# Score visits of three pairs instead of two in the first columns of a fused attention and feed-forward kernel

## The chip, the cores and the metric

The kernel runs on one core of a Trainium2 chip. The metric is the device time of one execution in microseconds (us); it is given as the median of five runs. A profile of one further execution shows each engine: PE is TensorE (its weight loads are listed apart as PEld), DVE is VectorE, ACT is ScalarE, POOL is GpSimd, and SP only issues DMAs here.

## The reference

Inputs: u and v with 8 batches x 3008 x 256, z with 8 x 3008 x 64, weights w_in (256 x 2048) and w_out (2048 x 256). Cut to what is computed:

```python
def _attn_ref(u, v, z):
    scores = (1.0 / S) * np.matmul(z, z.transpose(0, 2, 1))
    attn = np.maximum(scores, 0.0) ** 2
    return u * np.matmul(attn, v)

def _moe_ref(x, w_in, w_out):
    h = x @ w_in
    return (h * np.cos(h)) @ w_out

reference = _moe_ref(_attn_ref(u, v, z).reshape(B * S, D), w_in, w_out)
```

The scores of a batch are symmetric, and squared ReLU is applied to each of them by itself.

## The kernel before

**Tiling.** The 3008 tokens of a batch are 23 blocks of 128 and one of 64. Four blocks make a column of 512, so a batch has NC = 6 columns. The score tile (b, c, R) holds the scores of the four key blocks of group R against the 512 queries of column c. It is made in two pairs, p = 0 for the blocks k = 0, 1 and p = 1 for k = 2, 3. z is only 64 wide, so the transposed z (zT) holds two neighbouring blocks one above the other, and the two matmuls of a pair (L271) read opposite halves of the rows: they are half-high, 64x128, and run side by side. Each writes one PSUM bank of 512 fp32 columns. The pool ps_w (L196) has six such banks, used in rotation; the first transposes of z, the scores, the first matmuls of the second stage (L516) and its results (L533) all take their banks from it. The pool ps_acc has the other two, one for each half of the 256 values.

**From scores to products.** s_squares empties a bank with a ReLU into the fp16 ring rt (L191, three buffers of a pair each), and DVE squares a pair into one of 18 stores (L309). In the first three columns of the first batch, which the code calls direct, ACT does the ReLUs (L307), but DVE takes the last block of each tile, and one more in the very first (L305). Then av_chunk (L362) multiplies blocks of v with the squared scores into the two acc banks, three blocks or six full-high matmuls at a time. The last half block of 64 tokens is half-high too (av_half, L339) and is issued within a visit. finish (L389) multiplies the finished acc with the transposed u on DVE and so makes x, the input of the second stage.

**The second stage** goes by tiles of 512 tokens: h_quantum (L516) makes 128 of the 2048 features, ACT takes the cosine (L520), DVE multiplies (L523), and y_quantum (L533) multiplies with w_out.

**Direct columns.** Later columns reuse the symmetry: a tile with R < c is the transposed tile (R, c), turned by a DMA on SP (turn_s, L321), and part of the products goes through sums (product, L482). The direct columns need none of that, since all six tiles of each are computed. They start with the diagonal, in the order R = c, c+1, ... around the six groups. TURNS (L247) lists when those of their tiles that later columns need are turned.

**What sets the order.** Every piece of work is put on a list with a planned time: `at(t, rank, f)`. One column is U = 8 units. The list is sorted and run through once, and that is the order in which PE's matmuls execute: `chain` ties each to the one before. The order on the other engines is the framework's, within the dependencies. A score visit (s_visit) issues all matmuls of its pairs, with av_half between where one is due, and then their evictions. The loop at L572 plans the visits of the direct columns; planned times also give each tile's store its lifetime (L596). The av chunks of column c are planned at c x 8 + q + 0.5, q = 0 to 7 (the last at 7.45 instead of 7.5).

**DMAs.** POOL issues the loads and SP the transposing DMAs, each queue in its own order. A load, and a transposition of u or z, is held until the matmul that came last on the list before it has executed (`hold`, L116). In the stretch in question these are: turn_u of column 0 (planned at 0.7, behind the first av chunk), turn_u of column 1 (1.5), load_u of column 2 (2.0), the quarters of w_in from 7 to 13 and of w_out at 19, 21, 23 and 25, and at 24 the z of the next batch.

**The start.** Eight matmuls on zeros (L716) run while z comes in. z is transposed on PE in three groups of eight blocks (first_z_turn, L222), planned at -30, -2.5 and 0.8, and copied to zT by ACT (L227, the first two groups) or DVE (L229, the third). The third group holds the blocks from 16 on, which the visits of R = 4 and 5 read.

Of the kernel before, what the change touches and what calls it, by code (L numbers as in the profile page):

```python
# [14 lines left out]
def kernel(  # L15
# [25 lines left out]
    NC = NJ // K  # L41
# [5 lines left out]
    U = 8  # L47
# [47 lines left out]
    slots = [kpool.tile([P, K * CW], FP16, name=f"s{i}") for i in range(NSLOT)]  # L95
    vsum = [kpool.tile([P, 4, 2, P], FP16, name=f"vsum{R}") for R in range(NW)]
    w_in16 = kpool.tile([P, NDH, Dff], FP16, name="w_in16")
# [50 lines left out]
    def load_v(b, g):  # L148
        t = vs(b, g)
        n, full, rest = rows(v, b, g)  # L150
        load(t[:, 0:n, :], full)
        if rest is not None:
            for p0 in (0, JLAST):
                load(t[p0:p0 + JLAST, n, :], rest)
# [12 lines left out]
    def load_u(b, c):  # L167
        r0 = c * CW
        n = min(K, (S - r0) // P)
        st = ust[c % 2]  # L170
        for dh in range(NDH):
            ds = slice(dh * P, (dh + 1) * P)
            load(
                st[:, dh, 0:n, :],
                u[b, r0:r0 + n * P, ds].rearrange("(j p) d -> p j d", p=P))
            if n < K:
                load(st[0:JLAST, dh, n, :], u[b, r0 + n * P:S, ds])
# [56 lines left out]

    def direct(b, c, R):


        return b == 0 and c <= 2

    def triangle(b, c, R):  # L240

        return R == c and (b, c) > (0, NC // 2)

# [14 lines left out]

    def s_matmuls(b, c, R, p):


        zt = zT[b % 2]
        banks = {}
        diagonal = triangle(b, c, R)
        for k in ((0, 1), (3, 2) if diagonal else (2, 3))[p]:
            s0 = k if diagonal else 0
            lo = 1 if k in ((1, 2) if diagonal else (1, 3)) else 0
            h = slice(lo * dqk, (lo + 1) * dqk)
            j0 = c * K + 1 - lo
            sp = ps_w.tile([P, CW], FP32, name="w")  # L270
            chain(nc.tensor.matmul(  # L271
                sp[:, s0 * P:], zt[h, R * K + k + 1 - lo, :],
                zt[h, j0 + s0:j0 + K, :].rearrange("p j w -> p (j w)"),
                start=True, stop=True))
            banks[k] = sp
        return banks
# [286 lines left out]
    scores = []  # L563
    when = {}
    for b in range(B):
        pairs = [(b, c, R, p) for c, R in groups for p in range(2)]
        for i in range(0, len(pairs), NV):
            some = [pr for pr in pairs[i:i + NV] if not direct(*pr[:3])]
            t = b * span - lead + span * i / len(pairs)
            if some:  # L570
                scores.append((2 * math.floor(t / 2) + 1.2, some))
        for c in range(NC):  # L572
            if direct(b, c, c):
                for i in range(NC):
                    R = (c + i) % NC
                    scores.append((c * U + 4 * i / 3 - 3.1, [(b, c, R, 0), (b, c, R, 1)]))
    for t, some in scores:
        for pr in some:
            when[pr[:3]] = max(t, when.get(pr[:3], t))
# [23 lines left out]
    for b in range(B):  # L603
        for R in range(NW):
            at(b * span + (TSUM[R] if b else 3 * U + 1 + 1.5 * R), 2, lambda b=b, R=R: v_sums(b, R))
        for c in range(NC):
# [4 lines left out]
            first, last = (0.6, 6.93) if d else (HALF[c] if W else 1.0, 7.3)  # L611
# [13 lines left out]
            elif W:  # L625
# [8 lines left out]
                for o, what in PLAN[c]:  # L634
                    for piece in what.split():
# [12 lines left out]
                        for j in part:  # L648
                            R = j // K
# [8 lines left out]
            for o, size in places:  # L658
                part = blocks[n:n + size]
                if part:  # L660
                    first, end = n == 0 and not W, n + size >= len(blocks)
                    at(o, 2, lambda b=b, c=c, part=part, first=first, end=end:
                       av_chunk(b, c, part, first, end))
                    for j in part:
                        R = j // K
# [6 lines left out]
    for m in range(NT):  # L672
        b, i = divmod((m + 1) * TW - 1, S)
# [10 lines left out]
    for b in range(B):  # L684
        t = b * span
        if b == 0:
            for g in range(NG):
                at(-100 + g, 0, lambda g=g: first_z_load(g))
                at((-30, -2.5, 0.8)[g], 0, lambda g=g: first_z_turn(g))
            first = [lambda: load_v(0, 0), lambda: load_u(0, 0), lambda: load_v(0, 1),  # L690
                     lambda: load_v(0, 2), lambda: load_u(0, 1)]
# [67 lines left out]
```

## Time and profile before

| | |
|---|---|
| time, median of 5 runs | 1214.65 us (1213.68 to 1214.69) |
| the profiled execution | 1221.56 us, of it the span from first to last instruction 1219.4 us |
| PE busy | 1208.2 us, 99% of the span |
| DVE busy | 1020.1 us, 84% |
| ACT busy | 831.5 us, 68% |
| POOL busy | 145.9 us, 12% |
| mean granted clock of TensorE | 0.997 |
| the visits' matmuls, L271, whole kernel | 684, 90.4 us |
| ReLUs on ACT of full tiles, L307 | 489, 613 ns each |
| squares of a pair on DVE, L309 | 254, 688 ns each |

The busy share of an engine counts time in which any instruction of it is under way. Neighbouring instructions overlap at their ends, so the distance from start to start is shorter than a duration: ACT starts ReLUs of 0.60 us every 0.48 us, DVE starts instructions of 0.68 us every 0.60 us. A line of a timeline or a chain has the start in us, the length in us, the engine, the source line, what it writes from what, and how many instructions are merged; in brackets stands the idle time before it and what ended that.

### The profile page before, as it was taken

To read this page: it belongs to the slowest core of one execution; us is meant where nothing else is said; L and a number is where in the kernel's file an instruction comes from. 1 tells how busy PE (TensorE), PEld (TensorE's weight loads), DVE (VectorE), ACT (ScalarE), POOL (GpSimd) and SP (SyncE) were. 2 spreads that over 40 slices of the span, in tenths; PEclk is the share of its full clock that TensorE was granted. 3 is DMA by queue.
4 is the path that set the end of the run, shared out by engine and by line. 5 is a ranking of instruction groups with operands and counts; after the bars stand their busy time and mean duration, and the time that the engine had idled before them with its cause. 6 is when DMAs were issued, how large, how long until landed. Compare 5 with 4: busy or idle time off the path is not lost.

```text
span 1219.4 us, 22944 instructions
## 1 busy us (share of the span) xinstructions
PE 1208.2 (99%) x8421; PEld 767.6 (63%) x8421; DVE 1020.1 (84%) x1995; ACT 831.5 (68%) x1741; POOL 145.9 (12%) x201
## 2 busy tenths in 40 slices
PE   8989999999999999999999999999999999999998
PEld 3346666666666666666666666666666666666666
DVE  8878988889888898888888888887888888888875
ACT  6757766677676777767767677776777767767545
POOL 3310101001010010100101001010010111100000
PEclk9989999999999999999999999999999999999999
DMA  9997968779687796858977679586695857956411
GB/s 151 189 153 115 141 104 123 124 120 142 98 121 120 127 136 108 121 111 125 128 121 122 110 120 154 103 124 107 113 154 102 132 102 111 160 94 120 73 31 49
DMA packets 484225, 145.02 MB, mean 119 GB/s; under 512 B 432400, under 2 KB 484112, under 8 KB 484112
## 3 DMA queue, kind: packets, MB, share of 16 engines
q1 hardware_dynamic: 356448, 88.73, 45.3%
q0 software_dynamic: 100400, 29.77, 24.8%
q10 hardware_dynamic: 27264, 25.06, 6.4%
q8 instruction: 66, 1.08, 0.4%
q14 instruction: 47, 0.39, 0.1%
HBM read 60.29 MB, written 24.64 MB: 70 GB/s over the span
## 4 chain that ended last, share of the span: by engine, by line
PE 94%; issue 2%; DMA 2%; DVE 1%; ACT 1%; POOL 0%; POOLq 0%; ACTq 0%; DVEq 0%
PE w L533 26%; PE w L516 25%; PE acc L482 18%; PE acc L362 18%; PE w L271 6%; DMA w_out<-in_moe_w_out_dram 1%; PE acc L339 1%; DMA v<-in_v_dram 1%; ACT rt L307 0%; PE w L716 0%; DVE g L523 0%; POOL zst L121 0%; DVE s L309 0%; DVE x L389 0%; ACT zT L227 0%
## 5 line engine op out<-in xcount | busy, mean ns | idle before, releaser
L520 ACT ACTIVATE c<-w 128x512 f16<-128x512 f32 x752 | 436.8, 620 | 262.2 <-PE w L516 215.2
L523 DVE TENSOR_TENSOR g<-w,c 128x512 f16<-128x512 f32 x752 | 492.4, 683 | 65.2 <-ACT c L520 63.5
L533 PE MATMUL w<-w_out,g 128*128 128x256 f16 x3008 | 448.9, 273 | 3.8 <-DMA w_out<-in_moe_w_out_dram 3.8
L516 PE MATMUL w<-x,w_in 128*128 128x512 f16 x1504 | 445.7, 379 | 0.0
L533 PEld LDWEIGHTS <-g 128*128 128x128 f16 x3008 | 294.5, 98 | 195.2 <-issue 4.4
L362 PE MATMUL acc<-s,v 128*128 128x512 f16 (+1 forms) x1024 | 293.0, 381 | 0.1
L307 ACT ACTIVATE rt<-w 128x512 f16<-128x512 f32 x489 | 253.1, 613 | 43.9 <-PE w L271 43.9
L309 DVE TENSOR_TENSOR s<-rt 128x1024 f16<-128x1024 f16 x254 | 172.7, 688 | 85.9 <-ACT rt L307 84.7
L516 PEld LDWEIGHTS <-w_in 128*128 128x128 f16 x1504 | 147.1, 98 | 73.5 <-issue 3.9
L482 PE MATMUL acc<-s,vsum 128*128 128x256 f16 (+1 forms) x1184 | 154.6, 270 | 0.2 <-DVE q L498 0.2
L121 POOL DMA_DIRECT2D ust<-in_u_dram x112 | 81.2, 731 | 563.5 <-PE acc L362 535.2
L362 PEld LDWEIGHTS <-v 128*128 128x128 f16 x1024 | 95.9, 98 | 79.6 <-issue 32.7
L482 PEld LDWEIGHTS <-vsum 128*128 128x128 f16 x1184 | 114.9, 98 | 18.4 <-issue 3.3
L482 PE MATMUL acc<-s,v 128*128 128x256 f16 (+1 forms) x888 | 115.1, 270 | 0.4 <-DVE x L389 0.4
L482 PEld LDWEIGHTS <-v 128*128 128x128 f16 x888 | 83.7, 98 | 19.8 <-issue 12.1
L451 DVE TENSOR_TENSOR s<-s,s 128x1024 f16<-128x1024 f16 (+1 forms) x148 | 92.8, 668 | 3.6 <-PE acc L482 3.6
L271 PE MATMUL w<-zT 64*128 64x512 f16 (+3 forms) x684 | 90.4, 359 | 2.4 <-ACT zT L227 1.6
L540 ACT ACTIVATE ob<-w 128x256 f32<-128x256 f32 x188 | 71.1, 378 | 12.6 <-PE w L533 12.6
L288 ACT ACTIVATE rt<-w 128x512 f16<-128x512 f32 (+3 forms) x176 | 62.8, 449 | 11.8 <-PE w L271 11.8
L121 POOL DMA_DIRECT2D v<-in_v_dram x40 | 31.2, 785 | 299.5 <-PE acc L482 146.5
L389 DVE TENSOR_TENSOR x<-acc,ut 128x512 f16<-128x512 f32 (+7 forms) x112 | 64.1, 596 | 2.2 <-PE acc L362 2.1
L441 DVE TENSOR_TENSOR s<-s 128x512 f16<-128x512 f16 (+1 forms) x148 | 60.0, 411 | 1.9
(37 smaller groups left out, 360.3 us busy)
## 6 DMA issues: line engine op xcount, KB each, us to landing
out_dram<-ob ACTq DMA_DIRECT2D x92, 256.0 KB, 2.4
ust<-in_u_dram POOLq DMA_DIRECT2D x80, 128.0 KB, 4.4
v<-in_v_dram POOLq DMA_DIRECT2D x16, 512.0 KB, 6.4
s<-s SPq DMA_TRANSPOSE x249, 4.4
v<-in_v_dram POOLq DMA_DIRECT2D x8, 448.0 KB, 9.3
zst<-in_z_dram POOLq DMA_DIRECT2D x14, 128.0 KB, 5.0
ust<-in_u_dram POOLq DMA_DIRECT2D x16, 96.0 KB, 5.0
w_in<-in_moe_w_in_dram POOLq DMA_DIRECT2D x4, 256.0 KB, 5.9
```

The costliest lines, as they stand in the source:

```text
L121: hold(nc.gpsimd.dma_start(dst, src))
L271: chain(nc.tensor.matmul(sp[:, s0 * P:], zt[h, R * K + k + 1 - lo, :], zt[h, j0 + s0:j0 + K, :].rearrange("p j w -> p (j w)"), start=True, ...
L307: nc.scalar.activation(rt[:, i, :], banks[k], AF.Relu)
L309: ins = nc.vector.tensor_tensor(t.rearrange("p s k w -> p k s w")[:, 2 * p:2 * p + 2], rv, rv, ALU.mult).ins
L362: chain(nc.tensor.matmul(acc[:, 0:wn], vs(b, j // G)[:, j % G, nh * P:(nh + 1) * P], a, start=(start and n == 0), stop=(last and n == len( ...
L451: after(nc.vector.tensor_tensor(dst, src, sub, ALU.subtract).ins, before[-1], NOSYNC)
L482: chain(nc.tensor.matmul(acc[bank][:, cols], lhs[:, k, :], rhs[:, k, :] if old else rhs[:, :, k * P:(k + 1) * P], start=(n in (1, 5) and i ...
L516: chain(nc.tensor.matmul(hp, w_in16[:, k, ft * P:(ft + 1) * P], x[:, k, :], start=(k == 0), stop=(k == NDH - 1)))
L520: nc.scalar.activation(c16, hp, AF.Sin, bias=math.pi / 2.0, scale=inv_s2)
L523: nc.vector.tensor_tensor(gs[(m, ft // FG)][:, ft % FG, :], hp, c16, ALU.mult)
L533: chain(nc.tensor.matmul(ys[m][:, 0:D], gs[(m, f4)][:, ft % FG, ts * P:(ts + 1) * P], w_out16[:, ft, :], start=(ft == 0), stop=(ft == NFT ...
L540: nc.scalar.activation(obs[m][:, i, :], ys[m][:, 0:D], AF.Copy, bias=0.0, scale=inv_s2)
```

## The change

The visits of the direct columns are no longer planned one tile at a time. All their pairs are put into one row, column after column, and cut into visits: the first has two pairs, the next ten have three, the last two have two.

```diff
-        for c in range(NC):
-            if direct(b, c, c):
-                for i in range(NC):
-                    R = (c + i) % NC
-                    scores.append((c * U + 4 * i / 3 - 3.1, [(b, c, R, 0), (b, c, R, 1)]))
+    pairs = [(0, c, (c + i) % NC, p) for c in range(NC) for i in range(NC) for p in range(2)]
+    pairs = [pr for pr in pairs if direct(*pr[:3])]
+    first = [0, 2, *range(5, 33, 3), 34]
+    for i, j in zip(first, first[1:] + [len(pairs)]):
+        scores.append((2 * i / 3 - 3.6, pairs[i:j]))
```

The planned times and contents that follow, with a pair written as (column, group, p):

| before | | after | |
|---|---|---|---|
| -3.10 | (0,0,0) (0,0,1) | -3.60 | (0,0,0) (0,0,1) |
| -1.77 | (0,1,0) (0,1,1) | -2.27 | (0,1,0) (0,1,1) (0,2,0) |
| -0.43 | (0,2,0) (0,2,1) | -0.27 | (0,2,1) (0,3,0) (0,3,1) |
| 0.90 | (0,3,0) (0,3,1) | 1.73 | (0,4,0) (0,4,1) (0,5,0) |
| 2.23 | (0,4,0) (0,4,1) | 3.73 | (0,5,1) (1,1,0) (1,1,1) |
| ... every 1.33 | one tile each | ... every 2.00 | three pairs each |
| 18.23 | (2,0,0) (2,0,1) | 17.73 | (2,0,0) (2,0,1) |
| 19.57 | (2,1,0) (2,1,1) | 19.07 | (2,1,0) (2,1,1) |

That makes 18 visits before and 13 after, of the same 36 pairs. The first av chunk (0.5) stands behind the third visit in both; the third group of z transposes (0.8) and the second chunk (1.5) come between the third and the fourth visit after the change, and on both sides of the fourth before it. The last half block of each direct column is still issued within a visit: those planned at 6.23, 12.90 and 19.57 before, at 5.73, 11.73 and 17.73 after. The last visit stood behind the chunk of 19.5 and directly ahead of the first h_quantum (20.0); it now stands ahead of that chunk. Nothing else is edited: the turns, the loads, the chunks and the numbers of banks and buffers keep their planned times and sizes.

## The prediction

> **What bounds the kernel now.** I read the page first, then the stretch that the change touches. The page's slices say that TensorE (PE) is busy nearly all the time, with one dent.
>
> ```profile
> PE   8989999999999999999999999999999999999998
> PEclk9989999999999999999999999999999999999999
> ```
>
> The dent (third slice, 61 to 91 us) lies behind the stretch that the change edits. A table of stretches splits that: 8.6 to 10.4 us is the start, 10.40 to 46.38 us runs from the first av chunk to the first quantum of the second stage (L516).
>
> ```profile
> 8.60:10.40 1.80, 1.06 (x4) 0.20 (x5) 1.80 (x4) 1.80 (x5) 1.59 (x4) 1.00 1.64 181
> 10.40:46.38 35.98, 35.90 (x192) 12.86 (x192) 32.42 (x54) 23.98 (x47) 7.21 (x10) 1.00 1.30 171
> ```
>
> The columns after the length are PE, its weight loads, VectorE (DVE), ScalarE (ACT), POOL, the granted clock and the DMA share. In the first row ACT and DVE are full and PE is not: the first scores wait for their evictions. In the second PE works 35.90 of 35.98 us, DVE 32.42, ACT 23.98: PE sets the pace, so a PE saving counts there, while DVE has 3.6 us to spare. The chain of waits shows what a visit costs PE:
>
> ```profile
> 12.37 0.54 PE w L271 x4
> 12.91 1.40 PE acc L362 x6
> 14.31 0.54 PE w L271 x4
> ...
> 53.82 1.29 PE acc L362 x6
> ...
> 116.88 0.75 PE w L271 x6
> ```
>
> Four half-high matmuls (two pairs) take 0.54 us, six take 0.75: a pair costs 0.21 and a visit 0.54 - 2 x 0.21 = 0.12 besides. The six full-high matmuls behind a visit take 1.40 us, six between other full-high ones 1.29: 0.11 more on leaving. So one visit costs 0.23 us of PE beyond its pairs.
>
> The timeline of the start, by engine:
>
> ```profile
> 8.93 3.08 ACT L307 ACTIVATE rt<-w 128x512 f16<-128x512 f32 x6
> 9.11 1.36 PE L271 MATMUL w<-zT 64*128 64x512 f16 x4 [0.54 <-ACT zT L227]
> 10.40 1.47 PE L362 MATMUL acc<-s,v 128*128 128x512 f16 x6
> 13.11 0.81 DVE L229 COPY zT<-w 128x1024 f16<-128x1024 f16 x2
> 24.11 1.28 DVE L389 TENSOR_TENSOR x<-acc,ut 128x512 f16<-128x512 f32 x2
> ```
>
> ACT empties a bank every 0.48 us (9.42, 9.90, 10.37 in narrower windows); DVE starts an instruction every 0.60 us; the first av chunk begins at 10.40.
>
> **The change part by part.**
>
> *Fewer visits.* 18 become 13, so five times 0.23 us: -1.15. The second and third visit stand side by side before the first chunk both before and after, so all five fall behind 10.40, where PE is full. Bounds: -1.15, and 0 should PE wait there instead.
>
> [...]
>
> *Two pairs moved ahead of the first chunk.* Before: three visits, six pairs. After: 2 + 3 + 3 = eight. Behind the chunk PE is spared 2 x 0.21 = -0.43. In front the third visit now holds (2,1), (3,0), (3,1), and all six banks are taken by the second. Its last matmul writes the bank that the ReLU of block (2,0), second half, reads: the fifth ReLU in the row of six from 8.93, so free at 8.93 + 4 x 0.48 + 0.60 = 11.45. Before, the last matmul before the chunk waited for the second ReLU, 8.93 + 0.48 + 0.60 = 10.01, and the chunk started 0.39 later. Add 0.35 (a visit's last pair to the next chunk): the chunk starts at 11.80, +1.40. Bounds: +0.95 if one ReLU goes to another place in ACT's order, +2.0 if one more stands ahead. The v transfer, awaited until 10.40 now, is no bound then.
>
> *What waits behind it.* Next on PE are the nine transposes of the third z group (L222), one chunk, and the visit of R = 4, which needs the zT copy on DVE (L229). The chain gives 11.80 + 1.40 + 0.50 + 1.30 = 15.00 for that visit (14.31 now). DVE, at 0.60 a start, has rt, square, square, rt, square after the rt of 11.31, so it is at 14.3 when the transposes, done about 13.85, want their copy: the copy ends at 15.0 if it goes next and at 15.6 if a square goes first. Nobody but PE waits for it. 0 to +0.6; I take +0.3, as nothing in the trace orders the two.
>
> *Bank and ring reuse in the steady part.* A visit is followed by two or three chunks, so the next starts 0.75 + 1.40 + 1.30 = 3.45 us later and finds all six banks last used by the visit before. A visit of kind A (two pairs of one block, one of the next) needs five ReLUs on ACT: from 0.42 us after its start (17.48 to 17.90 in the timeline), 0.42 + 4 x 0.48 + 0.60 = 2.94. Kind B (one, then two) gives DVE two bank-emptying maxima (L305) and three squares, 5 x 0.60 = 3.0 us, its last bank empty by 3.3 at the worst order. Both are under 3.45 plus the 0.4 until the third pair's turn: 0, and up to 0.3 a visit if DVE is behind. The rt ring (L191, three buffers) is just as deep as a visit; its third buffer is released by 3.65 and wanted at about 5.3.
>
> *End of a column.* The x multiplications (L389, 2 x 0.60) hold the two acc banks that the next chunk wants. For column 0 the third square of the visit before is ready at the same moment (2.95 us after its start) as the first x; if it goes first, PE waits 0.3. For column 1 x goes first, and a wait of 0.15 us seen now (the chain's chunk at 39.07, due at 38.92) goes. -0.15 to +0.3, taken as +0.05.
>
> *DMAs and queues.* The moved visits issue no DMA: the turns of these columns have times of their own (L247), and none precedes its squares. The gates shift: turn_u of column 0 on SP opens at the end of the first chunk, 11.90 now, 13.3 then. Behind it on SP stands turn_u of column 1, which starts only at 20.48 since its u has not landed; the transposed u is wanted at 24.11 and the staging buffer was free at 20.66. So 0. POOL's weight loads wait for matmuls that move by the net shift. The planner's slots (L587), worked through for the new times, are each reused only after the reader of the old content. The last direct visit moves ahead of one chunk (19.07 for 19.57); the next visit (21.2) still waits for the product of the last quantum before it: 0.
>
> Sum: -1.15 - 0.43 + 1.40 + 0.3 + 0.05 = **+0.17 us**. The profiled execution took 1221.56 us, its span 1219.4 and 2.2 around it; so 1221.7 for it. The median of the runs shown is 1214.65, 0.6% less, and the same sum gives 1214.8. From the bounds of the start, the copy and the column's end, this case runs from -1.15 - 0.43 + 0.95 - 0.15 = -0.8 to -1.58 + 2.0 + 0.6 + 0.3 = +1.3: 1213.9 to 1216.0.
>
> **The rivals.** The dent decides what could be larger. PE waits there for the last quarter of w_out, and its clock falls:
>
> ```profile
> 74.59 1.01 PE L533 MATMUL w<-w_out,g 128*128 128x256 f16 x4 [3.77 <-DMA w_out<-in_moe_w_out_dram]
> ...
> 75.40 4.90 PE L362 MATMUL acc<-s,v 128*128 128x512 f16 x11
> ```
>
> Eleven matmuls take 4.90 us and not 11 x 0.216 = 2.4, and four take 1.01 and not 0.44, so the halved clock costs about 3.0 and the dent 3.77 + 3.0 = 6.8 us. The profiled run is 1221.56 - 1214.65 = 6.9 us longer than the median; so the runs that count probably lack the dent.
>
> *Rival 1, slower: the clock falls at the start.* Place: 8.6 to 11.8 us, where PE, waiting for banks, now does six half-high matmuls (6 x 0.21 = 1.3 of 3.2 us). In the dent the clock fell about 3 us after PE's last matmul, and in 8.6 to 10.4 at 1.06 of 1.80 us it stayed 1.00. It decides when the sparse stretch counts as idle over its whole length. Price 3.0: 1214.8 + 3.0 = 1217.8. Against it: PE is never idle for over 0.6 us there.
>
> [...]
>
> *Rival 2, faster: the transfers shift.* SP issues the turned tiles one after another from 20.48 to 75.2 us, and w_out shares the DMA engines with them. The turn of (0,0,3) is ready some 1 us earlier relative to the turn_u that now goes ahead of it; if the order flips, SP uses its idle time before 20.48 for it, all later ones come up to 4.5 us (one issue, 21.82 to 26.45) sooner, and the dent's wait goes. If the median runs have the dent: 1214.8 - 6.8 = 1208.0. Against: the 6.9 us above, and the turn_u is still ready first by about 1 us.
>
> *Rival 3, slower: the dent comes into runs that lack it.* PE is early, or w_out late, by enough: 1214.8 + 6.8 = 1221.6. For it: the profile shows how little separates the two; against: the gate of w_out moves along with PE.
>
> *Rival 4: the full saving, start hidden.* If the start costs only its lower bound and no copy or x is late: 1213.9, within the same class.
>
> **How the numbers follow.** 0.2% is 2.4 us, about what a measurement of this kernel can tell from no change. Forecast with Rival 4: 0.50. Rival 1: 0.12. Rival 3: 0.10. DVE late at each of the eight three-pair visits from 1.73 on (0.3 x 8 = +2.4 and the sum, 1217.2): 0.09. Rival 2: 0.10, and other shifts of the transfers to the fast side 0.09. Faster 0.19, same 0.50, slower 0.31. The range takes in Rival 1 and the late DVE and stops short of Rivals 2 and 3: 1212.0 to 1218.6; the likeliest case alone has 1213.9 to 1216.0.
>
> **What would show it.** After the change: 13 rows of L271 before the first L516, ten of them 0.75 us; the first L362 at about 11.8; the first L516 at 46.2 to 47, with PE still full from the first chunk on; clock 1.00 until the dent. A first chunk before 11.3 or a clock under 1.00 at 12 us refutes the start; L271 rows over 0.9 us behind 15 us refute the bank reuse; a w_out wait of another length makes the prediction wrong whatever the rest does.

## The result, and the profile after

The changed kernel takes 1216.19 us (median of 26 runs, 1215.45 to 1217.46) where the kernel before takes 1214.66 (44 runs): the ratio is 1.0012, 95% interval 1.0007 to 1.0018. That is 1.5 us more, and within the 0.2% that was set as no change. The profiled execution took 1216.23 us with a span of 1214.2.

The page after, the two slice rows that showed the dent, and the rows of the table of stretches that answer to the two of before (start; first av chunk to first L516):

```profile
PE   8999999999999999999999999999999999999998
PEclk9999999999999999999999999999999999999999
```

```profile
6.20:11.70 5.50, 4.10 (x25) 1.33 (x25) 5.06 (x9) 4.94 (x9) 4.73 (x7) 0.94 1.43 170
11.70:48.83 37.13, 36.01 (x189) 13.90 (x188) 33.12 (x54) 23.30 (x46) 6.50 (x9) 0.96 1.33 184
```

The two rows of stretches list, behind the length, the busy time of PE, its weight loads, DVE, ACT and POOL, then the granted clock and the DMA share. The dent is gone from this execution. But the first chunk comes at 11.70 us, the first L516 at 48.83 where it was 46.38, and PE now has 1.1 us idle in the second stretch (36.01 of 37.13) and a mean clock of 0.96. The chain of waits shows the start of it:

```profile
10.61 1.16 PE w L271 x4
11.76 2.67 PE acc L362 x6
14.44 0.59 PE w L222 x9
15.03 1.29 PE acc L362 x6
16.32 0.75 PE w L271 x6
17.07 2.69 PE acc L362 x12
```

The first chunk's six matmuls take 2.67 us and not 1.40: 0.445 each, half speed. From 15.03 on everything has its old pace, and visits of six take 0.75. The clock in half-microsecond stretches (PE busy, clock, DMA share, GB/s) has the limits:

```profile
10.50:11.00 0.50, 0.39 (x3) 1.00 1.55 180
11.00:11.50 0.50, 0.50 (x2) 0.58 1.49 195
...
14.00:14.50 0.50, 0.50 (x5) 0.51 1.44 197
14.50:15.00 0.50, 0.50 (x10) 1.00 1.46 199
```

Halved from about 11.1 to 14.5 us. Three waits stand in the steady part, in PE's timeline:

```profile
26.39 0.82 PE L271 MATMUL w<-zT 64*128 64x512 f16 x6
27.51 2.75 PE L362 MATMUL acc<-s,v 128*128 128x512 f16 x12 [0.30 <-DVE x L389]
...
40.33 0.82 PE L271 MATMUL w<-zT 64*128 64x512 f16 x6
41.66 2.75 PE L362 MATMUL acc<-s,v 128*128 128x512 f16 x12 [0.52 <-DVE x L389]
44.35 0.61 PE L271 MATMUL w<-zT 64*128 64x512 f16 x4
45.26 0.39 PE L339 MATMUL acc<-s,v 64*128 64x512 f16 x2 [0.30 <-DVE s L309]
45.58 1.47 PE L362 MATMUL acc<-s,v 128*128 128x512 f16 x6
```

The first two are chunks that begin a column and find acc not yet read. The third is the half block of column 2. By the starts, each of these visits takes longer to its chunk than the 0.75 us of an undisturbed one: 27.51 - 26.39 = 1.12, 41.66 - 40.33 = 1.33 and 45.58 - 44.35 = 1.23. So PE loses 0.37, 0.58 and 0.48.

### The profile page after: what moved, and what is told of

Its sections match the earlier page's. It is cut to its first block, busy times and chain, and to the rows that moved or that the text cites. A ratio compares the mean times of both kernels' runs of the same rounds, so it can differ in the third digit from the quotient of the medians.

```text
span 1214.2 us, 22940 instructions
## 1 busy us (share of the span) xinstructions
PE 1205.5 (99%) x8421; PEld 767.3 (63%) x8421; DVE 1021.0 (84%) x1995; ACT 831.3 (68%) x1741; POOL 145.8 (12%) x201
## 4 chain that ended last, share of the span: by engine, by line
PE 98%; DVE 0%; DMA 0%; ACT 0%; issue 0%; ACTq 0%; DVEq 0%
PE w L533 27%; PE w L516 27%; PE acc L362 19%; PE acc L482 19%; PE w L271 6%; PE acc L339 1%; DMA g<-in_z_dram 0%; DVE s L309 0%; DVE x L389 0%; DVE rt L305 0%; ACT rt L307 0%; ACTq L209 0%; ACT zT L227 0%; DVE zst L217 0%; ACT c L520 0%
## 5 line engine op out<-in xcount | busy, mean ns | idle before, releaser
L516 PE MATMUL w<-x,w_in 128*128 128x512 f16 x1504 | 445.7, 379 | 0.0
L516 PEld LDWEIGHTS <-w_in 128*128 128x128 f16 x1504 | 147.0, 98 | 73.2 <-issue 3.1
```

Of the source, the lines that this page charges most:

```text
L516: chain(nc.tensor.matmul(hp, w_in16[:, k, ft * P:(ft + 1) * P], x[:, k, :], start=(k == 0), stop=(k == NDH - 1)))
```

## The experiments

The expectations weigh three theories of where the loss arises. A puts it at the start and in the halved clock there, B in the visits of three pairs of the steady part, C behind the first L516, in the transfers. (From ends on, the letters stand for what each expectation says.) One table first, since all runs are read by it. Times are from each profile's PE timeline: the first visit, the distances from there to the visit of R = 4 and from that to the first L516, and what is left of the span behind the first L516.

| profile | first visit | to R = 4 | to first L516 | behind it | median of its executions |
|---|---|---|---|---|---|
| before, second profile | 6.47 | 7.60 | 32.14 | 1165.4 | 1214.65 |
| before, third profile | 6.78 | 8.24 | 32.14 | 1165.3 | 1214.55 |
| changed | 6.22 | 10.03 | 32.58 | 1165.4 | 1216.19 |
| changed, second profile | 6.34 | 10.05 | 32.58 | 1165.3 | 1216.37 |
| warm | 6.78 | 9.02 | 32.58 | 1165.3 | 1215.89 |
| start_two | 6.31 | 7.72 | 33.20 | 1165.4 | 1215.76 |
| rest_two | 6.78 | 8.43 | 32.14 | 1172.6 | 1215.96 |
| ends | 6.59 | 10.10 | 31.28 | 1165.3 | 1215.41 |
| col_two | 6.78 | 7.60 | 32.09 | 1165.8 | 1216.27 |
| col_two_ends | 6.50 | 7.60 | 31.50 | 1165.5 | 1213.60 |
| best | 6.78 | 7.60 | 31.50 | 1165.5 | 1214.88 |
| before_wout | 6.78 | 8.24 | 32.14 | 1165.3 | 1214.78 |

The last column but one answers theory C at once: unless PE waits for w_out (rest_two), the time behind the first L516 is 1165.3 to 1165.8 us in every profile. What the front loses or gains arrives at the end, within 0.5 us. The distances repeat to about 0.1 us where the clock does the same, while the executions of one kernel scatter by 1 to 2 us and more, so I read the causes from the profiles and use the times only as a check.

**before_again**: nothing edited.

> The kernel before once more, for a second profile. If the halved clock and the wait for w_out behind 70 us belong to the one profiled execution only, the span here is about 1212.5 us, the clock stays 1.00 from 70 to 90 us and PE waits under 0.5 us for w_out; if they are in every execution, the span is about 1219 us. Time 1214.7 us, ratio 1.000 either way.

Span 1211.6 us, clock 1.00 throughout, no wait for w_out; ratio 1.0007 (0.9996 to 1.0017). The dent of the first profile belonged to that execution: of the 154 executions of before that stand beside these runs, five took over 1218 us. It is no part of the difference.

**warm**: ten full-high matmuls more, between the score pairs of the second and third visit.

```diff
+    def warm(n):
+        acc = ps_acc.tile([P, CW], FP32, name="acc")
+        for i in range(n):
+            chain(nc.tensor.matmul(acc, ident, zT[0][:, 0:4, :]..., start=True, stop=True))
...
+            if pair in WARM:
+                warm(WARM[pair])
```

> The changed kernel with ten more full-high matmuls (zT against the identity, into an acc bank that nobody reads) put between the score pairs of the second and third visit, where PE waits for banks. Theory A (the start costs the time, and 1.4 us of it is the clock that halves from 11.2 to 14.5 us in a stretch with little PE work): the clock stays 1.00 there, the first av chunk's six matmuls take 1.3 to 1.4 us and not 2.67, the visit of R = 4 stands 8.7 us behind the first visit and not 10.1, time 1214.8 us, 1.4 less than the changed kernel. Theory B (the loss arises from visits of three pairs in the steady part) and theory C (it arises behind the first L516, in the transfers): the start may come earlier, the time stays at 1216.2.

PE's timeline of it, from the last of the added matmuls (L330):

```profile
10.99 0.82 PE L330 MATMUL acc<-zT,ident 128*128 128x512 f16 x3
11.75 0.61 PE L271 MATMUL w<-zT 64*128 64x512 f16 x4
12.29 1.47 PE L375 MATMUL acc<-s,v 128*128 128x512 f16 x6
```

The first chunk (now L375) is at full speed, the clock is 1.00 in every stretch, and R = 4 comes 1.0 us sooner behind the first visit (9.02 for 10.03, where 8.7 was expected). The added matmuls cost some of it, as PE is busy all of 7.8 to 11.2 us, and PE also waits for the zT copy, which DVE runs behind two squares here:

```profile
15.80 0.82 PE L271 MATMUL w<-zT 64*128 64x512 f16 x6 [0.25 <-DVE zT L229]
```

The stretch to the first L516 is the same 32.58. The gain shows in the profile; in the medians it is only 0.3 us and not the expected 1.4 (1215.89, ratio to before 1.0016, 1.0008 to 1.0025). One profile can't show that the added matmuls kept the clock, since that of rest_two kept it without them; the executions lean that way, with 10 of 11 at a mean clock of 1.000 against 17 of 37 of the changed kernel.

**start_two** and **rest_two** undo one half each.

```diff
 start_two
-    first = [0, 2, *range(5, 33, 3), 34]
+    for i in range(4):
+        scores.append((4 * i / 3 - 3.1, pairs[2 * i:2 * i + 2]))
+    first = [*range(8, 33, 3), 34]
 rest_two
+    first = [0, 2, 5, 8]
+    for i, j in zip(first, first[1:]):
+        scores.append((2 * i / 3 - 3.6, pairs[i:j]))
+    for n in range(4, 18):
+        c, i = divmod(n, NC)
+        scores.append((c * U + 4 * i / 3 - 3.1, pairs[2 * n:2 * n + 2]))
```

> The changed kernel, but the first four visits as before (one tile of two pairs each, R = 0 to 3, at the planned times of before); three pairs from R = 4 on. Theory A: clock 1.00 at the start, the visit of R = 4 stands 7.7 us behind the first visit as before, the first L516 40.2 us behind it (39.7 before, 42.6 in the changed kernel, 0.5 of the difference from waits at the columns' ends), time 1215.1. Theory B: time 1216.2, as in the changed kernel. Theory C: anything from 1214.7 to 1216.2 that does not follow the first L516.

> The start of the changed kernel (visits of 2, 3 and 3 pairs before the first av chunk), and one tile of two pairs a visit from R = 4 on, as before. Theory A: the clock halves at the start as in the changed kernel, the visit of R = 4 stands 10.1 us behind the first, the first L516 42.1 us, time 1215.7. Theory B: time 1214.7, as before.

start_two: the start is as before (7.72, clock 1.00). The rest takes 33.20 and not the expected 32.5: the visit of R = 4 now stands one chunk behind the visit of R = 3 and waits for its banks.

```profile
14.03 0.82 PE L271 MATMUL w<-zT 64*128 64x512 f16 x5
15.10 0.37 PE L271 MATMUL w<-zT 64*128 64x512 f16 x1 [0.25 <-ACT rt L307]
15.41 2.76 PE L362 MATMUL acc<-s,v 128*128 128x512 f16 x12
```

1.38 us for a visit of 0.75, so 0.63 lost with only one chunk between two visits of three pairs. Ratio 1.0011 (1.0002 to 1.0020).

rest_two: the rest is as before to the hundredth (32.14). Its profiled start kept the clock (1.00 in every half microsecond from 7 to 15 us), against what I expected, and so gives the price of the start without it:

```profile
7.87 0.84 PE L271 MATMUL w<-zT 64*128 64x512 f16 x4
9.25 2.83 PE L271 MATMUL w<-zT 64*128 64x512 f16 x8 [0.54 <-ACT zT L227]
12.01 1.47 PE L362 MATMUL acc<-s,v 128*128 128x512 f16 x6
```

The chain of waits ahead of that chunk ends on ACT's fifth ReLU in the row that starts at 9.07:

```profile
10.98 0.68 ACT rt L307
11.66 0.04 issue
11.71 0.37 PE w L271
12.08 1.40 PE acc L362 x6
```

The first chunk is 12.01 - 6.78 = 5.23 us behind the first visit (3.76 before), R = 4 8.43 behind it. With the clock halved the changed kernel needs 10.03 and 10.05: 1.6 us more. In its executions the two show apart: five with a mean clock of 1.000 took 1214.8 to 1215.5, six with 0.998 or 0.999 took 1215.9 to 1216.8. Ratio 1.0007 (0.9994 to 1.0020). Theory B, that the loss is all in the steady part, falls: the rest alone undone doesn't restore the start, and the median stays at 1215.96 where B expected 1214.7.

**after_again**: the changed kernel once more.

> The changed kernel once more, for a second profile and more executions. [...]

The profile is again one with the halved clock; in 6 of its 11 and 14 of the 26 earlier executions the mean clock is below 1.000, as it is in 12 of the 110 executions of before beside the experiments. Ratio 1.0021 (1.0012 to 1.0030).

PE's work ahead of the drop doesn't explain by itself why rest_two kept the clock with the same first three visits. Times in us:

| profile | the stretch | PE busy in it | clock in it | clock behind it |
|---|---|---|---|---|
| changed | 7.8 to 11.2 | 2.12 of 3.40 | 0.98 | 0.50 (11.1 to 14.5) |
| changed, second profile | 7.8 to 11.2 | 2.46 of 3.40 | 1.00 | 0.53 (11.2 to 14.6) |
| before, second profile | 7.8 to 11.2 | 2.64 of 3.40 | 1.00 | 1.00 (10 to 20) |
| warm | 7.8 to 11.2 | 3.40 of 3.40 | 1.00 | 1.00 (11.2 to 14.6) |
| rest_two | 8.5 to 12.0 | 2.49 of 3.50 | 1.00 | 1.00 (12.0 to 15.0) |

The clock fell behind a stretch 0.62 and 0.72 full and held behind 0.78 and 1.00, but in rest_two it also held with 0.71. The profiles differ in the time before: the eight transposes ahead of the first visit take 1.06 us from 4.62 in rest_two and 0.62 from 4.50 in the changed kernel. Whether that decides it isn't shown.

**ends** takes the three waits away.

```diff
-            first, last = (0.6, 6.93) if d else (HALF[c] if W else 1.0, 7.3)
+            first, last = (2.0 if c == 2 else 0.6, 6.93) if d else (HALF[c] if W else 1.0, 7.3)
...
-            s_squares(*pair, banks)
+            if pair in LATE:        # (0, 1, 3, 0), (0, 2, 4, 0)
+                late.append((pair, banks))
+            else:
+                s_squares(*pair, banks)
...
             ended[:] = [ins]
+            while late:
+                s_squares(*late.pop())
```

> The changed kernel with two edits at the ends of columns: the last pair of the visit ahead of the end of columns 0 and 1 is squared behind the x multiplications, not ahead of them, and the half block of column 2 is issued in a later visit (21.2, not 17.73). Theory A (PE's waits there are DVE's order: 0.30 and 0.51 us for x, 0.55 at the half block): these three waits go, the stretch from the visit of R = 4 to the first L516 is 31.2 us and not 32.6, and the time is 1.3 less than the changed kernel's, 1214.9. Theory B (the waits cover something that is late anyway, such as the banks of the next visit): the stretch shortens by under 0.5, time 1215.8 or more.

The stretch is 31.28 and the three waits are gone. DVE's timeline ahead of column 1's end, first in the changed kernel, then in ends, where the line of x is L395:

```profile
38.85 1.29 DVE L309 TENSOR_TENSOR s<-rt 128x1024 f16<-128x1024 f16 x2 [0.18 <-ACT rt L307]
40.32 0.69 DVE L309 TENSOR_TENSOR s<-rt 128x1024 f16<-128x1024 f16 x1 [0.18 <-ACT rt L307]
40.93 1.28 DVE L389 TENSOR_TENSOR x<-acc,ut 128x512 f16<-128x512 f32 x2
42.13 1.27 DVE L305 TENSOR_SCALAR rt<-w 128x512 f16<-128x512 f32 x2
43.33 1.88 DVE L309 TENSOR_TENSOR s<-rt 128x1024 f16<-128x1024 f16 x3
```

```profile
39.05 1.29 DVE L309 TENSOR_TENSOR s<-rt 128x1024 f16<-128x1024 f16 x2 [0.17 <-ACT rt L307]
40.26 1.28 DVE L395 TENSOR_TENSOR x<-acc,ut 128x512 f16<-128x512 f32 x2
41.45 0.68 DVE L309 TENSOR_TENSOR s<-rt 128x1024 f16<-128x1024 f16 x1
```

In the changed kernel DVE is held at 40.32 by a square that waits for ACT, with x behind it in DVE's order; x then pushes the next maxima to 42.13 and their squares to 43.33, and the half block of column 2 reads one of these. In ends the late square no longer stands ahead of x. Against rest_two the stretch is 0.86 shorter with four visits fewer and the 0.15 us wait of before gone, so a visit less is worth (0.86 - 0.15) / 4 = 0.18 us, or 0.21 when the 0.12 that a visit at 30.27 waits is allowed for. Ratio 1.0014 (0.9999 to 1.0029): by the profile 1.3 us of the loss, in the times less, as three of its eleven executions took over 1218 us.

**col_two** and **col_two_ends** keep the start and column 0 as they were and use three pairs from column 1 on; the second also squares late as in ends. (Two small edits go along: the turn of (0,2,3) comes at 15.76, behind its tile, and a store's lifetime is counted from its own visit.)

```diff
-    first = [0, 2, *range(5, 33, 3), 34]
+    for i in range(NC):
+        scores.append((4 * i / 3 - 3.1, pairs[2 * i:2 * i + 2]))
+    first = [*range(12, 36, 3)]
     for i, j in zip(first, first[1:] + [len(pairs)]):
-        scores.append((2 * i / 3 - 3.6, pairs[i:j]))
+        scores.append((min(2 * i / 3 - 2.27, 19.07), pairs[i:j]))
```

> Column 0 as before (six visits of two pairs), columns 1 and 2 in visits of three: 14 visits for 18, with the start untouched. Theory A (a visit costs PE 0.23 us besides its pairs, and only the start and the columns' ends take this back): clock 1.00 at the start, the visit of R = 4 stands 7.7 us behind the first; four visits less give 0.92 back and the waits for x cost 0.66 more than before, so the first L516 stands 39.5 us behind the first visit (39.7 before), time 1214.4. Theory B (visits of three pairs cost PE time of their own): over 40.2 us, time 1215.2 or more.

> The same as col_two, with the last pair ahead of the end of columns 0 and 1 squared behind x. Theory A: no wait for x, four visits less (0.92) and the 0.15 us wait of before gone, so the first L516 stands 38.7 us behind the first visit, and the time is 1213.6, 1.0 less than before. Theory B: over 39.7 us behind it, time 1214.7 or more.

The first L516 stands 39.69 and 39.10 us behind the first visit (39.74 before). The start is untouched in both. col_two has the x waits (0.30 twice); col_two_ends has none, and misses its expected 38.7 mainly by the last visit, which has one chunk ahead of it and takes 1.13 us for 0.82. So four visits fewer bring 0.64 us in the profile. The times don't follow: ratios 1.0018 (1.0008 to 1.0027) and 0.9998 (0.9989 to 1.0007).

**col_two_ends_b** and **before_third**: repeats.

> col_two_ends once more, since its first interval (0.9989 to 1.0007) doesn't tell it from the kernel before. Theory A: the first L516 stands 0.6 us earlier behind the first visit than before (39.1 against 39.7), the time behind it is 1165.4 as in all undisturbed profiles, so the executions are 0.6 us shorter: 1213.0 where those of before are 1213.6, ratio 0.9995. If the earlier first L516 is given back behind it, the ratio is 1.000 or more.

> The kernel before a third time, for a profile of an execution of about 1214.65 us: its executions gather near 1213.6 and near 1214.65, and the second profile was one of 1213.68. If the 1.05 us lie ahead of the first L516, that comes at 47.2 us and not at 46.2 with 1165.4 us behind it; if they lie behind, it comes at 46.2 with 1166.4 behind it.

col_two_ends_b came out at 1.0021 (1.0003 to 1.0039). Its profile has the first L516 39.09 behind the first visit as expected, but also a wait (total, times, longest):

```profile
PE w L542 <- DMA w_out<-in_moe_w_out_dram: 4.9, 1, 4.9
```

and 1173.1 us behind the first L516: the dent again, in 5 of its 12 executions by their time (over 1220 us). Theory A's expectation of 0.9995 was wrong.

before_third explains the two groups of before. PE's timeline:

```profile
4.72 0.95 PE L222 MATMUL w<-ident,zst 128*128 128x128 f16 x7
6.78 1.03 PE L271 MATMUL w<-zT 64*128 64x512 f16 x4 [1.10 <-ACT zT L227]
7.75 1.04 PE L222 MATMUL w<-ident,zst 128*128 128x128 f16 x8
...
47.16 1.47 PE L516 MATMUL w<-x,w_in 128*128 128x512 f16 x6
```

The first visit takes 1.03 us and not 0.60, and the eight transposes behind it 1.04, where the changed kernel's second profile has 0.62. The first chunk, at 11.18, has its usual 1.47, so the slow pace ended before it. The first L516 comes at 47.16, 0.95 later than in the second profile, with 1165.3 behind it. That is the distance between 1213.68 and 1214.65, the two profiled executions; that all executions of before gather near 1213.6 and 1214.65 by how long the slow pace lasts is inferred from these two and the one of before_wout (first visit 1.03 us too, 1214.77).

**best** and **before_wout**: the last quarter of w_out ahead of the z loads on POOL, in col_two_ends and in before.

```diff
-                at(19 + 2 * q, 0, lambda q=q: load_w_out(q))
+                at(19 + 1.6 * q, 0, lambda q=q: load_w_out(q))
```

> col_two_ends with the quarters of w_out planned 1.6 units apart and not 2, so that POOL issues the last one ahead of the five z loads (some 4 us earlier). Theory A (an earlier first L516 is given back in some executions because PE then reaches the last quarter of w_out before it has landed, and the wait halves the clock): no wait for w_out, no execution of 1220 us, the first L516 at 39.1 behind the first visit, 1165.4 behind that, and executions near 1213.0 to 1214.2. Theory B (the long executions have another cause): executions of 1218 us and more remain as frequent as in col_two_ends (6 of 23).

> The kernel before with the same earlier quarters of w_out alone. Theory A: the executions of 1218 us and more go, the others stay at 1213.6 to 1215.1, median 1214.5, so the gain of the other run is its own. Theory B: no difference to before, long executions included.

POOL's timeline of best has it in the new order:

```profile
57.78 0.75 POOL L121 DMA_DIRECT2D w_out<-in_moe_w_out_dram x1 [3.03 <-PE w L271]
58.52 3.87 POOL L121 DMA_DIRECT2D zst<-in_z_dram x5
```

One of 12 executions took over 1218 us (6 of 23 in col_two_ends), none of 11 in before_wout, where the kernel before itself has only 5 of 154. That leans to theory A, but these are few, and the one that is left speaks against it. Ratios 1.0003 (0.9992 to 1.0014) and 0.9998 (0.9990 to 1.0007): no version tried here is shown to beat the kernel before.

## Why the prediction was right, and where it was not

The class and the range held: +0.17 us was forecast and +1.5 measured, a little beyond the +1.3 at which the likeliest case ended. Some of that is luck: the range was wide enough to take in Rival 1, and a clock drop that the sum left out came with about half of its price. By the prediction's own signs the start went otherwise, since the clock was 0.50 at 12 us, and the first L516 came at 48.83 and not at 46.2 to 47. Term by term, the distances of the profiles against the working:

- *Fewer visits, -1.15.* Right in kind, a little large: 0.18 to 0.21 us a visit for the 0.23 taken, so about -1.0. Once two chunks stood between visits, PE lost little to DVE's pace or to banks (one wait of 0.12 us in ends).
- *First chunk, +1.40.* Right: 5.23 - 3.76 = +1.47 in rest_two, 5.29 in the second profile of the changed kernel, from ACT's row of ReLUs as worked out. (In the first profile, 5.48, the cast of z came late, and the chain runs through a maximum on DVE instead.)
- *zT copy, +0.3.* 0: DVE's order has the copy ahead of the square, and neither the two profiles of the changed kernel nor that of rest_two, at full clock, shows PE waiting for it. In warm, with the squares first, PE waits 0.25, close to the +0.3.
- *Columns' ends, +0.05.* The step that failed. Measured 0.37 and 0.58 for x and 0.48 at the half block, less the old 0.15: +1.3. For column 0 the square went first, the case priced at 0.3. For column 1 I let x go first, and it was indeed ready first: ends shows it starting at 40.26, 2.76 behind its visit at 37.50, which from the changed kernel's visit at 37.31 is 40.07, ahead of the square of 40.32. But the square stood ahead of it in DVE's order, and x started behind it, at 40.93. And I carried the delay no further than x: the maxima of the next visit are tied behind x, their squares come later still, and the half block, issued two chunks on, reads one of them.
- *Rival 1, the halved clock.* It was put at 0.12 and 3.0 us. It came in about 54% of the executions (14 of 26 and 6 of 11, by a mean clock below 1.000), and costs 1.6 us at the same first visit (10.03 to 10.05 against 8.43). The price was taken from the dent, where the slow stretch lasted 6.8 us; here it lasts 3.4, so about half of that is lost. My argument against it, that PE is never idle for over 0.6 us there, was true (0.55 at most in both profiles) and decided nothing: PE was busy 2.46 of the 3.40 us from 7.8 to 11.2 in the second profile, and the clock fell. No run here shows what makes it fall.
- *Rivals 2 and 3, the dent.* Not needed for this result. The time behind the first L516 is the same in both kernels whenever the dent is absent, and of the 37 executions of the changed kernel one took over 1218 us. That the median runs of before lack the dent was right.

Summed from the profiles, the changed kernel reaches its first L516 0.83 us later by the start's banks, 1.6 by the clock and 0.44 by the rest (waits +1.3, four visits -0.85), less 0.25 for an earlier first visit: 2.6, as against the second profile of before (48.83 - 46.21). Against the third it is 1.7. The 1.5 of the medians is less than both, because both profiles of the changed kernel have the clock drop and not all executions do: 17 of the 37 have a mean clock of 1.000 and a median of 1215.73, 1.1 above before, and the other 20 have 1216.50, 1.8 above. So the banks and the columns' ends cost about 1.1 us in the times, and the clock adds about 0.8 where the distances give 1.6. Executions that keep the clock may start later, as rest_two's profile does (first visit at 6.78, against 6.22 and 6.34), but there is no profile of the changed kernel with the clock kept to show it.

What stays open: why the variants with three pairs from column 1 wait for w_out more often than the kernel before, although their first L516 is hardly earlier. Theory A, PE's arrival, doesn't explain it by itself. Nor does POOL's order: the last quarter goes out behind the five z loads in both, at 61.72 us in the second profile of before and at 61.58 in col_two_ends_b.

## What to carry to other kernels

Price a saving on the bounding engine from its own rows, and then walk each neighbour's queue in the order in which it will execute: a small saving can be eaten by one instruction that stands ahead of the awaited one and waits for something else. Work pulled ahead of a pipeline's first full stretch was paid for twice here, in the wait itself (+1.47 us in rest_two) and, in both profiles of the changed kernel, in the clock (1.6 us). And when executions of one kernel differ by as much as the change, compare distances between the same events in the profiles.

## What the runs showed of the hardware

- At the start of the changed kernel the granted clock fell to 0.50 from about 11.1 to 14.5 us, behind a stretch (7.8 to 11.2) in which PE was busy 2.12 of 3.40 us; in its second profile behind one with 2.46. It held with 2.64 (second profile of before) and 3.40 (warm), but also in rest_two with 2.49 of 3.50.
- In the first profile of before PE waited 3.77 us for w_out, ahead of the matmul at 74.59. The clock fell at about 73.5 us, 2.7 behind PE's last matmul, and stayed at 0.50 until about 80.4.
- The first visit of the same program takes 0.60 us in one profile and 1.03 in another (second and third profile of before), and its first L516 differs by 0.95 us between the two; the mean granted clock shows 1.00 in both.
- At an equal number of pairs, each visit less saved PE 0.18 to 0.21 us (ends against rest_two).
